# The distance bias of steps 14 to 35: from VectorE's pass over the scores to an identity matmul on PE

## The chip, the cores and the metric

The kernel runs on one core of one Trainium2 chip. The time is the device time of one execution in microseconds. The runs shown take 443.14, 443.22 and 443.57 us, median 443.22 us. The profiled execution took 443.25 us, and its span, from the first to the last instruction, is 441.4 us.

## The reference

A local attention with a few global keys is followed by a gated feed-forward layer with a convolution over time. Batch 4, 8 heads of 64, 768 positions, model width 512, inner width 1024:

```python
scores = scale * np.matmul(q, k.transpose(0, 1, 3, 2))        # scale = 1/8
keep = is_global | is_local                                   # 8 global keys, 96 local ones back
dist = np.where(is_global & ~is_local, float(n_local), np.abs(rel))
scores = scores - slopes[:, None, None] * dist                # slopes 2**-(head + 1)
scores = np.where(keep, scores, -1000000000.0)
a = np.exp(scores - scores.max(-1)); a = a / (a.sum(-1) + 1e-09); o = a @ v
h = np.maximum(x @ w_in, 0.0)                                 # x: the heads' o side by side
conv_out[t] = conv_w[0] * h[t - 1] + conv_w[1] * h[t] + conv_w[2] * h[t + 1]
out = h / (1 + np.exp(-conv_out)) @ w_out
```

`w_in`, `conv_w` and `w_out` come as float64 and are decoded on the chip into two fp32r planes, high and low.

## The kernel before

**Steps.** A batch's 768 queries are cut into two units `u` of 384, a unit into 3 blocks `i` of 128 queries. A job `m` is one pair of heads of one unit of one batch, 32 jobs in all (`jobs`, in the order batch, unit, pair), and a step `s` is one block of one job: 96 steps, `steps[s] = (m, i)`. A step's 128 queries see at most 232 keys (`WIN`: 96 before them, their own 128, 8 global ones); where `u` and `i` are both 0 (`first`) there are 128 (`W0`).

**One step.** `scores(s)` (line 353) writes both heads' scores into one PSUM bank, a tile `both` of 128 x 2 x 256, of which there are two that take turns (`ps_s`). In jobs 0 to 11 (`NATIVE`), which are steps 0 to 35, a head's scores are one fp32 matmul over 64 rows (line 365), which the chip runs as two instructions with a weight load each. Later jobs use planes of fp32r and two matmuls over 128 rows (line 375). `maxima(s)` (line 384) then runs one VectorE instruction per head (line 392): it adds the bias and mask from the table `tab`, multiplies by -0.125, writes the result over the scores, and gives the least value of each row, the negative of the maximum. A short instruction behind it reads the accumulator into `mm`. `exps(s)` (line 399) is one exponential per head on ACT, out of PSUM into a buffer in SBUF (`pbuf`, one of four), with `mm` as its bias and the sums as a by-product. `normalise` (line 417) multiplies by the inverse sums, mostly on POOL (line 427); `transposes` (line 429) turns the blocks on PE (lines 434 and 436) and copies them on ACT; `block` (line 475) multiplies them with the values.

**The table.** `tab` (line 189) holds, in bf16 for each of the 8 heads, 232 + 128 columns of bias times 8, with a very large negative number where a key is masked; `ident` (line 172) is the identity in fp32, used by the transposes.

**The feed-forward half.** `mm1` (line 523) and `mm2` (line 634) are its matmuls in fp32r, three products per tile. They stand in a queue, from which `fill` puts some into each step, so that PE has work besides the attention. Lines 569 to 571 are the convolution (POOL, then VectorE twice).

**Order.** Steps 0 to 13 (`HAND` is 14) are in an order written out by hand (`by_hand`), with warming matmuls in bf16 between them (line 152). From step 14 on a planner orders the instructions of every engine by estimated durations. In steps 14 to 29 (`alone`) the sums get their 1e-9 on POOL (line 420). POOL's queue at the start holds the masks' index tiles, the identity, then the distances (lines 200 and 201), which wait for VectorE, and the tables. At the end the kernel checks that its inputs lie in the range it was written for, and jumps to a general version if not; it isn't taken here.

Of the kernel before, what the change touches and what calls it, by code (L numbers as in the profile page):

```python
# [11 lines left out]
BF16 = mybir.dt.bfloat16  # L12
# [3 lines left out]
ALU = mybir.AluOpType  # L16
# [4 lines left out]
P = 128  # L21
# [4 lines left out]
NB = TB // P  # L26
NPREV, NGLOB = 96, 8
WIN = NPREV + P + NGLOB
# [12 lines left out]
HAND = 14  # L41
FREE = 4
NATIVE = 12
# [17 lines left out]
def key_start(u, i):  # L61
    return (P + NGLOB) * i - (0 if u or i == 0 else P + NGLOB - 32)
# [5 lines left out]
def fast_path(tc, io):  # L68
    nc = tc.nc
    V, A, G, T = nc.vector, nc.scalar, nc.gpsimd, nc.tensor  # L70
# [4 lines left out]
    def pool(name, bufs, **kw):  # L75
        p = tc.tile_pool(name=name, bufs=bufs, **kw)
        pools.append(p)
        return p.__enter__()

    const = pool("const", 1)  # L80
# [90 lines left out]
    G.iota(keyi, pattern=[[1, 64]], base=0, channel_multiplier=0)  # L171
    ident = const.tile([P, P], F32, name="ident")
    make_identity(nc, ident)
    V.tensor_copy(rel, reli)
    keepkey = p1.tile([P, NT + 64], F32, tag="ob", name="keep")
    keep, key = keepkey[:, :NT], keepkey[:, NT:]
# [12 lines left out]
    tab = const.tile([P, H, NT], BF16, name="tab")  # L189
# [151 lines left out]
        V.tensor_tensor(bad, bad, red[:, 1:2], ALU.add)  # L341

    steps = [(m, i) for m in range(len(jobs)) for i in range(NB)]
    last_ttr = {}
    st_s, st_pt, pv, xt, sums = {}, {}, {}, {}, {}

    def alone(s):
        return HAND <= s < NB * (NATIVE - 2)

    def free(s):  # L350
        return s < NB * FREE

    def scores(s):
        m, i = steps[s]
        b, u, hp = jobs[m]
        w = NKC[u]
        first = u == 0 and i == 0
        n = W0 if first else WIN
        k0 = key_start(u, i)
        both = ps_s.tile([P, 2, 256], F32, tag="s", name=f"s{s}")  # L360
        sp = [both[:, 0], both[:, 1]]
        for j in range(2):
            if m < NATIVE:
                rq, rk = raw[m]
                last_mm[s] = T.matmul(  # L365
                    sp[j][:, :n],
                    rq[:D, j * TB + i * P : j * TB + (i + 1) * P],
                    rk[:D, j * w + k0 : j * w + k0 + n],
                    start=True,
                    stop=True,  # L370
                )
                continue
            qh, ql, kk = qk[m]
            for n_, (q_, st, sp_) in enumerate(((qh, True, False), (ql, False, True))):
                last_mm[s] = T.matmul(  # L375
                    sp[j][:, :n],
                    q_[:, j * TB + i * P : j * TB + (i + 1) * P],
                    kk[:, j * w + k0 : j * w + k0 + n],
                    start=st,
                    stop=sp_,  # L380
                )
        st_s[s] = (sp, n, first)

    def maxima(s):
        m, i = steps[s]
        b, u, hp = jobs[m]
        sp, n, first = st_s[s]
        mm = p1.tile([P, 8], F32, tag="mm", name=f"mm{s}", bufs=6)
        for j in range(2):
            h = 2 * hp + j  # L390
            tb = tab[:, h, WIN:] if first else tab[:, h, 0:WIN]
            last_ttr[s] = V.tensor_tensor_reduce(  # L392
                out=sp[j][:, :n], in0=sp[j][:, :n], in1=tb,
                scale=-0.125, scalar=3.0e38, op0=ALU.add, op1=ALU.min,
                accum_out=mm[:, j : j + 1],
            )
        st_s[s] = (sp, n, mm)

    def exps(s):
        m, i = steps[s]  # L400
        sp, n, mm = st_s[s]
        pb = pbuf[s % NPB]
        total = mm[:, 2:4]
        if free(s):
            if i == 0:
                sums[m] = p1.tile([P, 4 * NB], F32, tag="sum", name=f"sum{m}", bufs=2)
            total = sums[m][:, 2 * i : 2 * i + 2]
        for j in range(2):
            last_exp[s] = A.activation(  # L409
                pb[:, j * WIN : j * WIN + n], sp[j][:, :n], AF.Exp,  # L410
                bias=mm[:, j : j + 1], scale=-1.0, accum_out=total[:, j : j + 1],
            )
        st_s[s] = (pb, n, mm)
        if s < SHARED and not alone(s) and not free(s):
            A.activation(mm[:, 4:6], mm[:, 2:4], AF.Identity, bias=eps)
# [288 lines left out]
    last_exp, last_mm, last_ev = {}, {}, {}  # L704
# [69 lines left out]
    def by_hand(s):  # L774
        m, i = steps[s]
        p, q = s - 1, s - 2
        scores(s)
        if q >= 0 and free(q):
            block(*steps[q])
# [6 lines left out]
        if p >= 0 and free(p):  # L786
            transposes(p)
        maxima(s)
        exps(s)
        if ends(s - 3):  # L790
            mixed_low((s - 3) // NB)
# [21 lines left out]
    for s in range(len(steps) + LAG_V + 1):  # L813
# [4 lines left out]
        else:  # L818
# [5 lines left out]
            if s < len(steps):  # L824
                scores(s)
                maxima(s)
                exps(s)
# [207 lines left out]
def build(nc, io):  # L1035
    with tile.TileContext(nc, schedule_with_timeline_sim=True) as tc:
        fast_path(tc, io)
# [50 lines left out]
```

## Time and profile before

| | |
|---|---|
| median of three runs | 443.22 us |
| profiled execution | 443.25 us, span 441.4 us |
| PE, matmuls | 434.3 us busy, 98% of the span |
| PE, weight loads | 375.1 us, 85% |
| VectorE | 345.1 us, 78% |
| ACT | 284.7 us, 65% |
| POOL | 221.9 us, 50% |
| native scores, line 365 | 144 matmuls, steps 0 to 35, 6.8 to 112.6 us |
| bias and maxima, line 392 | 192, 73.1 us busy, mean 382 ns |
| exponentials, line 409 | 192, 82.7 us busy, mean 439 ns |

A matmul's busy time lasts until its modelled end, which lies well behind the start of the next one; what a matmul costs is therefore read from start to start. The weight loads have a row of their own, since they run beside the matmuls before them. An instruction's idle time is put down to what ended it last.

### The profile page before, as it was taken

The numbers are of one execution on the slowest core, as the hardware profiler recorded it, in microseconds if no ns is written. First come the engines' busy times: TensorE is split into PE (matmuls) and PEld (weight loads), VectorE is DVE, ScalarE is ACT, GpSimd is POOL, SyncE is SP. The second block draws the span as 40 slices with busy tenths as digits, with TensorE's granted clock in tenths as the row PEclk, the third lists the DMA queues.
The fourth block names the chain that finished last, engine by engine and source line by source line (L and its number), as shares of the span: only waits on it lengthen the run. The fifth ranks groups of instructions, "written<-read, shape, count | busy, mean of one in ns | idle before, by whom it ended". The sixth has DMA issues, their size and how long they took to land.

```text
span 441.4 us, 8881 instructions
## 1 busy us (share of the span) xinstructions
PE 434.3 (98%) x3014; PEld 375.1 (85%) x3014; DVE 345.1 (78%) x888; ACT 284.7 (65%) x771; POOL 221.9 (50%) x324
## 2 busy tenths in 40 slices
PE   9999999999999999999999999999999999999996
PEld 8677877788879998889989988889989998799885
DVE  5797899979999988857989897857989876666600
ACT  2777698597887875747776676647776675336311
POOL 4311789954834963557656873557656731022000
PEclk9999999999999999999999999999999999999999
DMA  7976855222243334253335234353334366810111
GB/s 218 311 214 192 244 170 166 75 82 84 91 134 131 110 111 133 73 166 105 108 117 164 85 109 134 97 154 98 112 110 135 131 228 231 287 55 1 48 50 53
DMA packets 20837, 58.70 MB, mean 133 GB/s; under 512 B 2736, under 2 KB 2992, under 8 KB 20784
## 3 DMA queue, kind: packets, MB, share of 16 engines
q1 hardware_dynamic: 16960, 51.56, 37.5%
q10 hardware_dynamic: 3824, 6.49, 3.9%
q8 instruction: 26, 0.43, 0.4%
q14 instruction: 27, 0.22, 0.2%
HBM read 51.75 MB, written 6.29 MB: 132 GB/s over the span
## 4 chain that ended last, share of the span: by engine, by line
PE 81%; DVE 7%; POOL 3%; DMA 3%; ACT 3%; issue 1%; SPq 0%; ACTq 0%; DVEq 0%; POOLq 0%
PE o L634 28%; PE h L523 26%; PE pv L485 7%; PE s L375 6%; PE t L434 4%; PE s L365 3%; PE t L436 3%; POOL pbuf L427 2%; DMA wr<-in_w 2%; DVE c L571 2%; DVE s L392 1%; DVE c L570 1%; PE o L904 1%; DMA rq<-in_qk 1%; PE warm L152 1%
## 5 line engine op out<-in xcount | busy, mean ns | idle before, releaser
L427 POOL TENSOR_SCALAR pbuf<-pbuf,mm 128x232 f32<-128x232 f32 (+1 forms) x156 | 108.0, 703 | 82.8 <-DVE mm L421 59.5
L409 ACT ACTIVATE pbuf<-s,mm 128x232 f32<-128x232 f32 (+1 forms) x192 | 82.7, 439 | 52.3 <-DVE mm L392 39.3
L392 DVE CUSTOM_DVE_ANT_0 s<-s,tab 128x232 f32<-128x232 f32 (+1 forms) x192 | 73.1, 382 | 10.2 <-PE s L365 4.0
L634 PE MATMUL o<-woh,gh 128*128 128x512 f32 x184 | 75.4, 410 | 0.0
L634 PE MATMUL o<-wol,gh 128*128 128x512 f32 x184 | 73.3, 398 | 0.0
L634 PE MATMUL o<-woh,gl 128*128 128x512 f32 x184 | 72.9, 397 | 0.0
L569 POOL TENSOR_SCALAR c<-hbuf,cw 128x382 f32<-128x382 f32 (+1 forms) x64 | 47.7, 748 | 47.1 <-ACT hbuf L533 25.0
L439 ACT ACTIVATE pt<-t 128x512 f32<-128x512 f32 (+1 forms) x96 | 53.9, 565 | 12.6 <-PE t L436 10.2
L523 PE MATMUL h<-xh,wih 128*128 128x384 f32 x252 | 59.5, 349 | 0.0
L523 PE MATMUL h<-xl,wih 128*128 128x384 f32 x252 | 57.6, 343 | 0.0
L523 PE MATMUL h<-xh,wil 128*128 128x384 f32 x252 | 56.5, 343 | 0.0
L570 DVE SCALAR_TENSOR_TENSOR c<-hbuf,cw,c 128x382 f32<-128x382 f32 (+1 forms) x64 | 46.4, 732 | 11.2 <-POOL c L569 11.2
L434 PE MATMUL t<-ident,pbuf 128*128 128x128 f32 x192 | 47.1, 275 | 0.3 <-ACT pt L439 0.2
L523 PEld LDWEIGHTS h<-xh,wih 128*128 128x128 f32 x252 | 43.2, 189 | 3.0 <-issue 1.5
L523 PEld LDWEIGHTS h<-xh,wil 128*128 128x128 f32 x252 | 43.5, 188 | 1.7 <-issue 1.2
L571 DVE SCALAR_TENSOR_TENSOR c<-hbuf,cw,c 128x382 f32<-128x382 f32 (+1 forms) x64 | 44.3, 693 | 0.6
L523 PEld LDWEIGHTS h<-xl,wih 128*128 128x128 f32 x252 | 43.1, 189 | 1.4 <-issue 0.9
L533 ACT ACTIVATE hbuf<-h 128x384 f32<-128x384 f32 x64 | 31.1, 493 | 17.9 <-PE h L523 17.8
L485 PEld LDWEIGHTS pv<-pt,v 128*64 128x64 f32 (+1 forms) x664 | 34.0, 136 | 9.5 <-issue 5.6
L589 ACT ACTIVATE c<-c 128x764 f32<-128x764 f32 (+1 forms) x32 | 27.2, 851 | 22.7 <-DVE c L571 19.8
L485 PE MATMUL pv<-pt,v 128*64 128x128 f32 (+1 forms) x664 | 40.9, 268 | 0.5 <-ACT pt L439 0.4
L634 PEld LDWEIGHTS o<-woh,gl 128*128 128x128 f32 x184 | 34.6, 188 | 7.9
(121 smaller groups left out, 851.0 us busy)
## 6 DMA issues: line engine op xcount, KB each, us to landing
v<-in_vv SPq DMA_DIRECT2D x32, 384.0 KB, 3.9
wr<-in_w SPq DMA_DIRECT2D x16, 512.0 KB, 4.6
check<-in_w SPq DMA_DIRECT2D x16, 512.0 KB, 4.6
rq<-in_qk SPq DMA_DIRECT2D x20, 384.0 KB, 3.1
rk<-in_qk SPq DMA_DIRECT2D x12, 504.0 KB, 3.7
out<-ob ACTq DMA_DIRECT2D x23, 256.0 KB, 2.5
rk<-in_qk SPq DMA_DIRECT2D x8, 400.0 KB, 3.3
rq<-in_qk SPq DMA_DIRECT2D x11, 192.0 KB, 5.4
```

The costliest lines, as they stand in the source:

```text
L392: last_ttr[s] = V.tensor_tensor_reduce(out=sp[j][:, :n], in0=sp[j][:, :n], in1=tb, scale=-0.125, scalar=3.0e38, op0=ALU.add, op1=ALU.min, ...
L409: last_exp[s] = A.activation(pb[:, j * WIN : j * WIN + n], sp[j][:, :n], AF.Exp, bias=mm[:, j : j + 1], scale=-1.0, accum_out=total[:, j : ...
L427: G.tensor_scalar(x, x, inv, 1.0, ALU.mult, ALU.mult)
L434: T.transpose(pt[:, 0, j], pb[:, j * WIN : j * WIN + P], ident)
L439: last_ev[s] = A.activation(sb[:, :k], pt[:, :k], AF.Copy)
L485: T.matmul(pv[m][64 * j : 64 * j + 64, i * P + q : (i + 1) * P], vt[m][:n, i, c, 64 * j : 64 * j + 64], sb[:n, c, j, q:], start=c == 0, st ...
L523: T.matmul(ps[:, :TB], w_[:, k, fs], x_, start=part == 0 and k == 0, stop=part == 2 and k == NK - 1,)
L533: A.activation(half, ps[:, :TB], AF.Relu, scale=0.5)
L569: G.tensor_scalar(c, *tap(1), 1.0, ALU.mult, ALU.mult)
L570: V.scalar_tensor_tensor(c, *tap(0), c, ALU.mult, ALU.add)
L571: V.scalar_tensor_tensor(c, *tap(2), c, ALU.mult, ALU.add)
L634: T.matmul(ps, g_[:, f], w_[:, f], start=f == 0 and part == 0, stop=f == NF - 1 and part == 2,)
```

## The change

In steps 14 to 35 (`added`) the head's score matmul no longer closes the sum in PSUM. Behind it stands a bf16 matmul of the 128 x 128 identity with the head's columns of `tab`, which adds the table to the scores and closes it: two such matmuls a step, of 232 columns, or 128 in steps 24, 27, 30 and 33. VectorE then takes the maximum of both heads in one reduction over 128 x 2 x n out of PSUM, writes no scores back, and multiplies the two maxima by -0.125 in a second, tiny operation. The exponentials read the sums in PSUM with a scale of 0.125 in place of -1. The identity in bf16 is copied from the fp32 one by POOL at the start.

```diff
--- before.py
+++ after.py
@@ -171,6 +171,8 @@
     G.iota(keyi, pattern=[[1, 64]], base=0, channel_multiplier=0)
     ident = const.tile([P, P], F32, name="ident")
     make_identity(nc, ident)
+    ident16 = const.tile([P, P], BF16, name="ident16")
+    G.tensor_copy(ident16, ident)
     V.tensor_copy(rel, reli)
     keepkey = p1.tile([P, NT + 64], F32, tag="ob", name="keep")
     keep, key = keepkey[:, :NT], keepkey[:, NT:]
@@ -341,8 +343,11 @@
         V.tensor_tensor(bad, bad, red[:, 1:2], ALU.add)
 
     steps = [(m, i) for m in range(len(jobs)) for i in range(NB)]
-    last_ttr = {}
+    last_ttr, whole = {}, {}
     st_s, st_pt, pv, xt, sums = {}, {}, {}, {}, {}
+
+    def added(s):
+        return HAND <= s < NB * NATIVE
 
     def alone(s):
         return HAND <= s < NB * (NATIVE - 2)
@@ -367,8 +372,13 @@
                     rq[:D, j * TB + i * P : j * TB + (i + 1) * P],
                     rk[:D, j * w + k0 : j * w + k0 + n],
                     start=True,
-                    stop=True,
+                    stop=not added(s),
                 )
+                if added(s):
+                    c0 = WIN if first else 0
+                    last_mm[s] = T.matmul(
+                        sp[j][:, :n], ident16, tab[:, 2 * hp + j, c0 : c0 + n], start=False, stop=True
+                    )
                 continue
             qh, ql, kk = qk[m]
             for n_, (q_, st, sp_) in enumerate(((qh, True, False), (ql, False, True))):
@@ -380,12 +390,20 @@
                     stop=sp_,
                 )
         st_s[s] = (sp, n, first)
+        if added(s):
+            whole[s] = both
 
     def maxima(s):
         m, i = steps[s]
         b, u, hp = jobs[m]
         sp, n, first = st_s[s]
         mm = p1.tile([P, 8], F32, tag="mm", name=f"mm{s}", bufs=6)
+        if added(s):
+            st_s[s] = (sp, n, mm)
+            both = whole.pop(s)
+            V.tensor_reduce(mm[:, 2:4], both[:, :, :n], axis=mybir.AxisListType.X, op=ALU.max)
+            last_ttr[s] = V.tensor_scalar(mm[:, 0:2], mm[:, 2:4], -0.125, None, ALU.mult)
+            return
         for j in range(2):
             h = 2 * hp + j
             tb = tab[:, h, WIN:] if first else tab[:, h, 0:WIN]
@@ -408,7 +426,8 @@
         for j in range(2):
             last_exp[s] = A.activation(
                 pb[:, j * WIN : j * WIN + n], sp[j][:, :n], AF.Exp,
-                bias=mm[:, j : j + 1], scale=-1.0, accum_out=total[:, j : j + 1],
+                bias=mm[:, j : j + 1], scale=0.125 if added(s) else -1.0,
+                accum_out=total[:, j : j + 1],
             )
         st_s[s] = (pb, n, mm)
         if s < SHARED and not alone(s) and not free(s):
```

## Rows read from the trace of the kernel before

**Rows 1.** Chain by engine (page part 4), then by line from 130 us.

```profile
PE 81%; DVE 7%; POOL 3%; DMA 3%; ACT 3%; issue 1%; SPq 0%; ACTq 0%; DVEq 0%; POOLq 0%
...
by line: PE o L634 39.7%; PE h L523 32.6%; PE pv L485 8.6%; PE s L375 8.2%; PE t L434 4.2%; PE t L436 3.6%; PE o L904 1.8%; ACT oc L908 0.1%; PE total L917 0.0%; issue 0.0%
```

**Rows 2.** Busy us by stretch: PE, PEld, DVE, ACT, POOL (instructions); granted clock; DMA.

```profile
44.00:113.00 69.00, 68.19 (x452) 54.97 (x453) 61.82 (x170) 53.39 (x158) 52.02 (x78) 1.00 0.46 143
113.00:130.00 17.00, 16.66 (x109) 14.10 (x110) 16.38 (x36) 14.11 (x37) 9.26 (x12) 1.00 0.26 77
130.00:390.00 260.00, 260.00 (x1813) 231.84 (x1812) 216.32 (x539) 171.97 (x460) 143.77 (x189) 1.00 0.42 137
```

**Rows 3.** Waits on PE, 44-441 us, matmuls and weight loads: us, times, longest.

```profile
PE t L436 <- POOL pbuf L427: 0.4, 1, 0.4
...
PEld s L365 <- ACT pbuf L409: 1.1, 4, 0.4
```

**Rows 4.** PE in time order, a native step and what follows: start, us.

```profile
62.06 0.46 PE L365 MATMUL s<-rk,rq 64*128 64x232 f32 x1
...
62.37 0.55 PE L365 MATMUL s<-rk,rq 64*128 64x232 f32 x2
...
62.56 0.55 PE L365 MATMUL s<-rk,rq 64*128 64x232 f32 x2
...
62.76 0.36 PE L365 MATMUL s<-rk,rq 64*128 64x232 f32 x1
63.04 0.44 PE L523 MATMUL h<-xh,wih 128*128 128x384 f32 x1
...
63.33 0.50 PE L523 MATMUL h<-xh,wih 128*128 128x384 f32 x2
```

**Rows 5.** PE in order of time, where bf16 matmuls stand beside others.

```profile
7.97 0.36 PE L365 MATMUL s<-rk,rq 64*128 64x232 f32 x1
...
8.26 0.51 PE L152 MATMUL warm<-setup 128*128 128x128 bf16 x6
...
22.40 0.33 PE L544 MATMUL h<-xh,wil 128*128 128x384 f32 x1
22.57 0.51 PE L152 MATMUL warm<-setup 128*128 128x128 bf16 x6
22.92 0.28 PE L434 MATMUL t<-ident,pbuf 128*128 128x128 f32 x1
...
41.97 0.22 PE L152 MATMUL warm<-setup 128*128 128x128 bf16 x1
42.12 0.46 PE L365 MATMUL s<-rk,rq 64*128 64x232 f32 x1
```

**Rows 6.** PE in time order, an fp32r score and the group behind.

```profile
116.11 0.28 PE L375 MATMUL s<-kk,ql 128*128 128x232 f32 x1
116.22 0.86 PE L523 MATMUL h<-xl,wih 128*128 128x384 f32 x4
...
116.22 0.34 PE L523 MATMUL h<-xl,wih 128*128 128x384 f32 x1
```

**Rows 7.** VectorE in time order, then groups by form: busy us, mean ns.

```profile
50.58 0.41 DVE L392 CUSTOM_DVE_ANT_0 s<-s,tab 128x232 f32<-128x232 f32 x1 [1.82 <-PE s L365]
...
51.08 0.41 DVE L392 CUSTOM_DVE_ANT_0 s<-s,tab 128x232 f32<-128x232 f32 x1
...
L392 DVE CUSTOM_DVE_ANT_0 s<-s,tab 128x232 f32<-128x232 f32 x160 | 63.7, 400 | 7.8 <-PE s L365 3.5 <-PE s L375 2.1 <-POOL tab L205 0.8
...
L421 DVE RECIPROCAL mm<-mm 128x2 f32<-128x2 f32 x84 | 13.3, 159 | 3.0 <-POOL mm L420 1.4 <-ACT mm L415 0.9
...
L333 DVE TENSOR_REDUCE misc<-acc 128x1 f32<-128x512 f32 x1 | 0.7, 687 | 0.0
```

**Rows 8.** ACT in order of time, the first exponential of step 16.

```profile
51.64 0.45 ACT L409 ACTIVATE pbuf<-s,mm 128x232 f32<-128x232 f32 x1 [1.26 <-POOL c L569]
```

**Rows 9.** POOL in order of time, its first operation on the masks' distances.

```profile
7.50 0.38 POOL L200 TENSOR_SCALAR keep<-loc 128x232 f32<-128x232 f32 x1 [5.22 <-DVE loc L199]
```

## The prediction

> **What bounds the kernel now.** I read the chain of waits first, then the busy time by stretch, then PE's waits, then single instructions in the stretch of steps 14 to 35. The chain [rows 1] is 81% PE with 7% of VectorE and 3% each of POOL and ACT; the pieces that are not PE lie ahead of 130 us, so the chain alone would let one think that VectorE or POOL sets the pace in the steps that are changed. The busy time by stretch says otherwise [rows 2]. From 44 to 113 us, where the scores of steps 14 to 35 run, PE is busy 68.19 of 69.00 us, VectorE 61.82, POOL 52.02. From 113 to 130 us PE is busy 16.66 of 17.00 us, and from 130 to 390 us all 260 us. PE's idle time from 44 to 390 us is thus 0.81 + 0.34 = 1.15 us. The waits of PE's matmuls from 44 us to the end agree: the longest is 0.4 us [rows 3]. PE has ready work of the feed-forward half to put in wherever a score or a transpose is late, so the last instruction comes when PE's list is done. What is added to PE's list after 44 us comes out at the end, less what it fills of 1.15 us of idle time.
>
> PE's busy time is modelled, so the price of an instruction is read from start to start of neighbours. One step of native scores with 232 columns [rows 4]: its four matmuls (two per head) start at 62.06, 62.37, 62.56 and 62.76, the next group's first two at 63.04 and 63.33. The gaps are 0.31, 0.19, 0.20, 0.28 and 0.29 us. The middle ones, 0.19 to 0.20, are the matmul itself. The others are longer: the first by 0.11, the fourth by 0.09, and the fifth by 0.12 against the 0.17 at which matmuls of that form follow one another (from 116.22, four of them in 0.86 us, each lasting 0.34: three gaps in 0.52) [rows 6]. What distinguishes those places is the form of the tile: the native scores are 64\*128 (64 rows of the array), their neighbours 128\*128. It isn't the type: from an fp32r matmul to a bf16 one, both 128\*128, the gap is 0.17 (22.40 to 22.57), and six bf16 pairs and the step to an fp32 transpose take 0.35 together, 0.058 each [rows 5]. But from a 64-row score to a bf16 128\*128 matmul it is 0.29 (7.97 to 8.26), and from a bf16 one to a 64-row score 0.15 (41.97 to 42.12) in place of 0.058 [rows 5]. So a change between 64 and 128 rows costs 0.09 us before it and some 0.11 us at the first pair behind it, unless that one is bf16 (the six from 8.26 take 0.51, the last of them 0.22: 0.058 from one to the next).
>
> The Trainium skill has a rule for this: TensorEngine Tiling (Array Packing), section Key Properties, says that changing the tiling mode, not merely the tile, drains the engine. It gives no figure; the trace agrees, at 0.09 us a change. It speaks against this change, whose identity has 128 rows and stands between scores of 64.
>
> **PE's part.** Each of the 22 steps gets two bf16 matmuls, identity by table. 18 steps have 232 columns, 4 (steps 24, 27, 30, 33) have 128. A bf16 pair of 128 columns takes 0.058 [rows 5]; 104 columns more at the granted clock of 1.00, the upper level of 2.4 GHz [rows 2], are 0.043, so 0.10, and the fp32r pairs of 232 columns that already run take 0.11 [rows 6]. From a step's first score to the second matmul behind the step:
> before 0.31 + 0.19 + 0.20 + 0.28 + 0.29 = 1.27;
> after 0.31 (head 0) + 0.29 (to the identity) + 0.19 (0.10 and 0.09 back to 64 rows) + 0.31 (head 1, its first weights exposed again) + 0.29 (to the identity) + 0.11 (to the next group, no change of form) + 0.17 = 1.67.
> The difference is 0.40 us. With 128 columns it is 0.40 - 2 x 0.043 = 0.31. The sum is 18 x 0.40 + 4 x 0.31 = 8.4 us. Bounds: 4.4 us if the changes of form cost nothing (36 x 0.11 + 8 x 0.058); at the most 8.4 + 22 x 0.11 = 10.8 us, if the first pair behind each step still pays as it does now. I take 8.4, since each of its gaps is a row with the same two forms.
>
> What it fills: PE's own idle time from 44 to 113 us, 0.81 us. VectorE, POOL and ACT get 8 us more for the same work, so I let PE's waits there go: -0.8. As lower bound, none of it goes; as upper, the 1.15 us.
>
> **VectorE's part.** Off: two maxima per step, 0.40 us each with 232 columns [rows 7], 0.82 to 0.91 for the pair back to back (50.58 to 51.08, and 0.41). On: one reduction over 464 columns. The nearest row is a reduction of 512 columns from SBUF, 0.687; 464/512 of it is 0.62, and I take 0.64, between the two. And a 128x2 scalar operation, 0.16 like the reciprocal of that size [rows 7]. Together 0.80 (0.78 to 0.85) where the pair had 0.80 to 0.91: VectorE loses 0.05 or gains 0.13 us a step, likely 0.1, some 2 us in all. That is off the path, as PE's idle time is what it could remove: already counted.
>
> **What becomes later.** The first maximum could start when head 0's second matmul had ended, 0.31 + 0.36 = 0.67 after the step's first one, and the pair ended 0.50 + 0.41 behind that, at 1.58; the exponentials followed the second maximum (51.08 + 0.41, and 51.64) [rows 7, 8]. Now the reduction waits for the second identity, which starts 0.31 + 0.29 + 0.19 + 0.31 + 0.29 = 1.39 after the first matmul and lasts some 0.27; with 0.80 for both operations the exponentials can start at 2.46, 0.9 later. Behind them stand the inverse, POOL's normalising and the transposes, three steps on, and the score bank: two banks turn, so the scores of step s+2 wait for the exponentials of s. That wait occurs 4 times now, 1.1 us of weight-load idle time in all [rows 3]. If each of the four were 0.9 longer it would be 3.6 us; but two steps of PE also become 2 x 0.40 = 0.8 longer, which covers nearly all of it. I take 0, with 3.6 as the upper end.
>
> **The rest.** POOL's copy of the identity to bf16 stands ahead of an operation before which POOL sits idle for 5.22 us [rows 9]: nothing. The planner orders everything from step 14 on anew from its own costs; it can't shorten PE's list, only shift where PE waits: 0, within about 1 us either way, by the 1.15 us that there is now. No DMA is added or moved past a queue. Sum: +8.4 - 0.8 = +7.6 us on the profiled execution's 443.25 us (span 441.4), 0.03 above the runs' median of 443.22: 450.9.
>
> **Rivals.**
> Columns only: the array takes the identity without the price of the form, between heads as well; 4.4 - 0.8 gives 446.9. For it: the bf16 pairs in a row cost their columns only. Against: both mixed gaps of rows 5. The Trainium skill's page TensorE: Matmul & The Clock Gate, section Back-to-back issue gap, would have it so: columns over 2.4 GHz plus 2.5 ns, an estimate of 0.099 and 0.056 us, 4.0 us in all; the rows of 64-row neighbours contradict it here.
> Faster, because VectorE sets the pace: if the chain's VectorE pieces are the true path from 44 to 130 us, the pairs on PE fall into time in which PE only does work ahead, and VectorE's 22 x 0.1 us come off: 441.0. It needs about 8 us of slack on PE ahead of 130 us; rows 2 show 1.15. It decides if modelled ends hide idle time in PE's busy.
> No change: POOL's normalising (75% busy from 44 to 113 us) sets the pace, PE's price is hidden and VectorE's gain too: 443.2. Against: the same 1.15 us.
> Late banks: the longer way to the exponentials stops PE at the score banks: 450.9 + 3.6 = 454.5.
>
> **How the numbers follow.** Full price 0.66 (449.5 to 452.5), columns only 0.13, late banks 0.06, faster 0.09, no change 0.06. The predicted time is that of the first, 450.9. The range, 446.6 to 453.4, takes in the second and leaves out the others, 0.21. Within 0.2% (0.9 us) is about what a measurement of this kernel can tell from no change. Faster 0.09, same 0.06, slower 0.85.
>
> **What would show it.** In a changed step the gap from a score to the identity should be 0.29, from the identity to head 1's first score 0.19, and 0.31 behind that; from the second identity to the next group 0.11. Step 36's last score, now at 116.11 [rows 6], should start some 7 to 8 us later, and everything behind it keep its length, with PE still busy all of its time. Reductions should take 0.62 to 0.69 us. I am wrong if these gaps stand near 0.10, if PE's list grows by 8 us and the end does not move, or if PE shows long waits for exponentials.

## The result

The changed kernel takes 449.60 us (median of four runs, 449.50 to 450.31), the kernel before 443.39 us (443.14 to 443.68, the runs beside it among them): a ratio of 1.0146, 95% interval 1.0133 to 1.0159, some 6.2 us slower. The profiled execution took 449.50 us, span 447.7 us; 6.25 us more than the one before.

### The profile page after: what moved, and what is told of

The parts are those of the page before. It is cut to its first block, busy times and chain, and to the rows that moved or that the text cites. A ratio compares the mean times of both kernels' runs of the same rounds, so it can differ in the third digit from the quotient of the medians.

```text
span 447.7 us, 8935 instructions
## 1 busy us (share of the span) xinstructions
PE 441.9 (99%) x3058; PEld 377.0 (84%) x3058; DVE 345.3 (77%) x844; ACT 285.0 (64%) x771; POOL 224.3 (50%) x325
## 4 chain that ended last, share of the span: by engine, by line
PE 95%; DMA 3%; ACT 1%; DVE 0%; issue 0%; SPq 0%; ACTq 0%
PE h L542 30%; PE o L653 29%; PE pv L504 8%; PE s L370 7%; PE s L385 6%; PE t L453 5%; PE t L455 4%; PE s L379 2%; DMA wr<-in_w 2%; PE o L923 1%; DMA rq<-in_qk 1%; PE warm L152 1%; PE h L563 1%; PE spare L504 1%; PE warm L479 1%; ACT pt L458 0%
## 5 line engine op out<-in xcount | busy, mean ns | idle before, releaser
L446 POOL TENSOR_SCALAR pbuf<-pbuf,mm 128x232 f32<-128x232 f32 (+1 forms) x156 | 106.4, 692 | 86.0 <-DVE mm L440 55.8
L588 POOL TENSOR_SCALAR c<-hbuf,cw 128x382 f32<-128x382 f32 (+1 forms) x64 | 49.4, 776 | 48.6 <-ACT hbuf L552 26.3
L410 DVE CUSTOM_DVE_ANT_0 s<-s,tab 128x232 f32<-128x232 f32 (+1 forms) x148 | 56.8, 385 | 8.8 <-PE s L385 5.1
L589 DVE SCALAR_TENSOR_TENSOR c<-hbuf,cw,c 128x382 f32<-128x382 f32 (+1 forms) x64 | 45.4, 717 | 10.0 <-POOL c L588 10.0
L590 DVE SCALAR_TENSOR_TENSOR c<-hbuf,cw,c 128x382 f32<-128x382 f32 (+1 forms) x64 | 43.3, 681 | 0.5
```

The source lines that it names most:

```text
L410: last_ttr[s] = V.tensor_tensor_reduce(out=sp[j][:, :n], in0=sp[j][:, :n], in1=tb, scale=-0.125, scalar=3.0e38, op0=ALU.add, op1=ALU.min, ...
L446: G.tensor_scalar(x, x, inv, 1.0, ALU.mult, ALU.mult)
L588: G.tensor_scalar(c, *tap(1), 1.0, ALU.mult, ALU.mult)
L589: V.scalar_tensor_tensor(c, *tap(0), c, ALU.mult, ALU.add)
L590: V.scalar_tensor_tensor(c, *tap(2), c, ALU.mult, ALU.add)
```

## The profile after

The chain by engine (page part 4), which answers to [rows 1]:

```profile
PE 95%; DMA 3%; ACT 1%; DVE 0%; issue 0%; SPq 0%; ACTq 0%
```

Then busy time by stretch, as in [rows 2] (PE, PEld, VectorE, ACT, POOL; granted clock; DMA), and the weight loads' wait that answers to [rows 3]; from 44 us on there is no wait of a PE matmul left to show:

```profile
44.00:113.00 69.00, 69.00 (x461) 51.55 (x459) 57.12 (x118) 49.94 (x143) 45.83 (x73) 1.00 0.42 125
113.00:130.00 17.00, 17.00 (x110) 13.93 (x106) 16.85 (x33) 13.34 (x40) 12.59 (x13) 1.00 0.35 107
130.00:390.00 260.00, 260.00 (x1818) 231.48 (x1817) 215.72 (x544) 174.93 (x469) 148.25 (x193) 1.00 0.42 135
```

```profile
PEld s L370 <- ACT pbuf L427: 0.4, 2, 0.2
```

PE is now busy all of the time from 44 to 390 us, and the chain is PE alone but for the start. The 1.15 us of idle time are gone.

One changed step of 232 columns on PE in order of time (line 370 the scores, 379 the identities, 542 the feed-forward half), which answers to [rows 4], and the last score of step 36, which answers to [rows 6]:

```profile
52.46 0.66 PE L370 MATMUL s<-rk,rq 64*128 64x232 f32 x2
53.05 0.27 PE L379 MATMUL s<-tab,ident 128*128 128x232 bf16 x1
53.25 0.66 PE L370 MATMUL s<-rk,rq 64*128 64x232 f32 x2
53.84 0.27 PE L379 MATMUL s<-tab,ident 128*128 128x232 bf16 x1
53.88 0.60 PE L542 MATMUL h<-xh,wih 128*128 128x384 f32 x2
...
125.30 0.27 PE L385 MATMUL s<-kk,ql 128*128 128x232 f32 x1
```

The first identity starts 0.59 behind the step's first score: 0.30 and 0.29. From there to head 1's first score it is 0.20, then again 0.59 to the second identity. The feed-forward group's first two start 0.04 and 0.30 behind that (two in 0.60, the last lasting 0.34). Step 36's last score moved from 116.11 to 125.30.

VectorE, by form and in order of time, answering to [rows 7]: the reduction (line 404), the scalar operation (405), and what stands behind each:

```profile
L404 DVE TENSOR_REDUCE mm<-s 128x2 f32<-128x464 f32 x18 | 11.4, 633 | 6.6 <-PE s L379 6.5
...
L405 DVE TENSOR_SCALAR mm<-mm 128x2 f32<-128x2 f32 x22 | 5.3, 241 | 0.3
...
54.41 0.63 DVE L404 TENSOR_REDUCE mm<-s 128x2 f32<-128x464 f32 x1
54.96 0.61 DVE L589 SCALAR_TENSOR_TENSOR c<-hbuf,cw,c 128x382 f32<-128x382 f32 x1
...
56.14 0.16 DVE L405 TENSOR_SCALAR mm<-mm 128x2 f32<-128x2 f32 x1
56.21 0.87 DVE L310 TENSOR_TENSOR wil<-w,wih 128x512 fp32r<-128x512 f32 x1
```

The reduction holds the queue for 0.55 (54.41 to 54.96), the scalar operation for some 0.07 where other work lies between. In the kernel before, a maximum with other work behind it held it for 0.32, so the pair for 0.64:

```profile
55.16 0.40 DVE L392 CUSTOM_DVE_ANT_0 s<-s,tab 128x232 f32<-128x232 f32 x1
...
55.48 0.68 DVE L308 TENSOR_TENSOR wil<-w,wih 128x512 fp32r<-128x512 f32 x1
```

With 0.62 for 0.64, VectorE's list got no shorter to speak of.

From the first score of step 14, which starts at 42.12 us in both traces, to the last matmul it is 395.02 us before and 401.36 after. Summing the gaps from start to start by the group that the earlier matmul belongs to (all of PE's matmuls, as in the fence above):

| PE from step 14 on, us | before | after | |
|---|---|---|---|
| native scores, 88 | 20.72 | 24.52 | +3.80 |
| identities, 44 | 0 | 5.26 | +5.26 |
| transposes, 312 | 31.17 | 29.73 | -1.45 |
| feed-forward, first half, 759 | 140.80 | 139.81 | -1.00 |
| feed-forward, second half, 599 | 139.23 | 138.99 | -0.24 |
| values, fp32r scores, the rest | 63.09 | 63.06 | -0.04 |

The list gained 9.06 us where the steps are. Priced by the step it is the same: from the first score to the second matmul behind the step it is 1.68 where it was 1.26 with 232 columns, and 1.29 where it was 0.92 with 128, so 18 x 0.42 + 4 x 0.37 = 9.0. And 2.7 us went from gaps of other groups, most of it waits, such as the 0.67 from one transpose to the next at 66.15 us of the kernel before, where 0.11 is usual. The busy times show 0.40 of that 0.56 as idle:

```profile
66.15 0.27 PE L434 MATMUL t<-ident,pbuf 128*128 128x128 f32 x1
66.82 0.33 PE L436 MATMUL t<-ident,pbuf 128*128 128x128 f32 x1 [0.40 <-POOL pbuf L427]
66.98 0.27 PE L434 MATMUL t<-ident,pbuf 128*128 128x128 f32 x1
67.09 0.27 PE L436 MATMUL t<-ident,pbuf 128*128 128x128 f32 x1
```

## Experiments

The theory after the result: PE's list sets the end; the changes between 64 and 128 rows are the larger half of what it gained; VectorE's part lies off the path (it does not move the end). The first rival: it isn't the form, but any further matmul in the sum. The second: VectorE's relief is what gave the 2.7 us back.

**1. Zero weights of 128 rows, VectorE as before**

```diff
# against the kernel before; nil16 is a 128 x 128 tile of bf16 zeros
-                    stop=True,
+                    stop=not added(s),
                 )
+                if added(s):
+                    c0 = WIN if first else 0
+                    last_mm[s] = T.matmul(
+                        sp[j][:, :n], nil16[:P], tab[:P, 2 * hp + j, c0 : c0 + n],
+                        start=False, stop=True,
+                    )
```

> The kernel before, with VectorE's two maxima as they were, and behind each head's scores of steps 14 to 35 a bf16 matmul of 128 rows by the same table columns as in the change, whose weights are zero: it adds nothing. PE's list is the changed kernel's, VectorE's that of before. Theory (PE's list sets the end, the changes between 64 and 128 rows are more than half of what it gained, VectorE is off the path): 449.6 us, 448.8 to 450.4, with gaps of 0.29 from a score to the added matmul and 0.20 from it to the next score. Rival (VectorE's relief is what gave back the 2.7 us that PE's other groups lost in the changed kernel): 451 to 452.3 us.

Measured: 449.69 us, ratio 1.0149 (1.0132 to 1.0166). One step on PE, where 379 is the added matmul:

```profile
52.50 0.66 PE L370 MATMUL s<-rk,rq 64*128 64x232 f32 x2
53.09 0.27 PE L379 MATMUL s<-tab,nil 128*128 128x232 bf16 x1
53.29 0.66 PE L370 MATMUL s<-rk,rq 64*128 64x232 f32 x2
53.88 0.27 PE L379 MATMUL s<-tab,nil 128*128 128x232 bf16 x1
53.92 0.95 PE L534 MATMUL h<-xh,wih 128*128 128x384 f32 x4
```

The gaps are those of the changed kernel, and so is the time, with VectorE's work untouched. PE's other groups lost 3.0 us here: 1.35 in the feed-forward's first half, 1.30 in the transposes, 0.38 in the second half. So PE's longer list is enough to give back the 2.7 us, and the second rival falls.

**2. The same with 64 rows**

```diff
# against run 1
-                        sp[j][:, :n], nil16[:P], tab[:P, 2 * hp + j, c0 : c0 + n],
+                        sp[j][:, :n], nil16[:D], tab[:D, 2 * hp + j, c0 : c0 + n],
```

> As the run with zero weights of 128 rows, but the added matmuls take only rows 0 to 63 of the zero weights and of the table, so that they have the scores' own form, 64*128. Number, columns, type and place in the sum are the same. Theory (the form is what costs): gaps of 0.20 from a score to the added matmul, 0.10 to 0.20 from it to the next score, no second 0.30; 0.2 to 0.3 us a step in place of 0.42; 444.7 to 446.7 us. Rival (any further bf16 matmul that adds to an fp32 sum costs this, whatever its rows): 449.6 us, as with 128 rows.

Measured: 445.72 us, ratio 1.0060 (1.0043 to 1.0076), 4.0 us less than with 128 rows, for the same number of matmuls, columns and types.

```profile
51.79 0.66 PE L370 MATMUL s<-rk,rq 64*128 64x232 f32 x2
52.28 0.26 PE L379 MATMUL s<-tab,nil 64*128 64x232 bf16 x1
52.38 0.56 PE L370 MATMUL s<-rk,rq 64*128 64x232 f32 x2
52.79 0.26 PE L379 MATMUL s<-tab,nil 64*128 64x232 bf16 x1
52.98 0.97 PE L534 MATMUL h<-xh,wih 128*128 128x384 f32 x4
```

From head 0's second score to the added matmul it is now 0.20 (51.79 and 0.30 and 0.20), from that to head 1's first score 0.10, and the gap behind, which was 0.30, is 0.21. The added matmul costs its columns; the 0.09 is paid once, behind the second one (52.79 to 52.98). The form is the cause, and the first rival falls. A step's gaps grew by 0.21 here (with 128 columns by 0.16), some 4.4 us in all, of which 2.5 show in the time.

The 0.10 agrees with what the Trainium skill's page TensorE: Matmul & The Clock Gate, section Back-to-back issue gap, gives as the gap of an isolated matmul: 0.099 for 232 columns, an estimate by it; run 1, where the form changes behind the same matmul, has 0.20. Runs 1 and 2 also agree with the rule of the Trainium skill's page TensorEngine Tiling (Array Packing), section Key Properties, that a change of tiling mode drains the engine: they show what a change costs, 0.09 to 0.10 us, and not the draining itself.

**3. One identity for both heads, ahead of the scores**

```diff
# against the changed kernel; the identities behind the scores are taken out
+        if added(s):
+            c0 = WIN if first else 0
+            T.matmul(
+                both[:, :, :n], ident16, tab[:, 2 * hp : 2 * hp + 2, c0 : c0 + n], start=True, stop=False
+            )
-                    start=True,
-                    stop=not added(s),
+                    start=not added(s),
+                    stop=j == 1 or not added(s),
```

> The changed kernel with one identity matmul over both heads' 464 columns, put ahead of the two scores, which add to it: as many columns as in the change, but no change of form between the heads, only the two per step that there were before. VectorE as in the change. Theory: PE gains about 0.19 to 0.22 us a step, 4.0 us in all, and its other groups lose up to 2.7 as they did: 444.4 to 447.4 us. Rival (the added columns and loads cost the same wherever they stand): 449.6 us.

Measured: 444.85 us, ratio 1.0038 (1.0025 to 1.0050).

```profile
51.79 0.37 PE L369 MATMUL s<-tab,ident 128*128 128x464 bf16 x1
52.09 1.05 PE L375 MATMUL s<-rk,rq 64*128 64x232 f32 x4
53.07 0.97 PE L542 MATMUL h<-xh,wih 128*128 128x384 f32 x4
```

As many columns as in the change; the identity takes 0.30 with the change to the scores in it, of which 0.20 is new (ahead of it stood the same change). The order, with one matmul for two, is worth 4.8 us, and the change still loses.

**4. Two reductions in place of one**

```diff
# against the changed kernel
-            V.tensor_reduce(mm[:, 2:4], both[:, :, :n], axis=mybir.AxisListType.X, op=ALU.max)
+            for j in range(2):
+                V.tensor_reduce(mm[:, 2 + j : 3 + j], sp[j][:, :n], axis=mybir.AxisListType.X, op=ALU.max)
```

> The changed kernel, but the maxima of steps 14 to 35 are two reductions of 232 columns, one per head, in place of one of 464. PE's list is the same; VectorE gets about 0.2 us more per step, 4 us in all. Theory (VectorE is off the path): 449.6 us, 448.9 to 450.4. Rival (the one reduction is worth its time): 451 to 453 us.

Measured: 449.53 us, ratio 1.0140 (1.0124 to 1.0157): as the changed kernel. The reductions, by form:

```profile
L405 DVE TENSOR_REDUCE mm<-s 128x1 f32<-128x232 f32 x36 | 12.7, 390 | 6.6 <-PE s L379 6.4
```

Two of 390 ns for one of 633 do not move the end, and no gain of the one reduction shows in this kernel. The test is a small one, though: from start to start the two hold VectorE for 0.62 where the one holds it for 0.55, so the run added 0.07 us a step, 1.5 us in all, and not the 4 that were expected.

**5. No change of form at all: scores over 128 rows, without identities**

```diff
# against the kernel before; wide(m): 5 <= m < NATIVE and m % NPAIR
-        n = D if m < NATIVE else P
+        n = D if m < NATIVE and not wide(m) else P
...
+                K = P if wide(m) else D
...
-                    rq[:D, j * TB + i * P : j * TB + (i + 1) * P],
-                    rk[:D, j * w + k0 : j * w + k0 + n],
+                    rq[:K, j * TB + i * P : j * TB + (i + 1) * P],
+                    rk[:K, j * w + k0 : j * w + k0 + n],
...
-            tb = tab[:, h, WIN:] if first else tab[:, h, 0:WIN]
+            k = h - 1 if wide(m) else h
+            tb = tab[:, k, WIN:] if first else tab[:, k, 0:WIN]
...
-                scale=-0.125, scalar=3.0e38, op0=ALU.add, op1=ALU.min,
+                scale=-0.0625 if wide(m) else -0.125, scalar=3.0e38, op0=ALU.add, op1=ALU.min,
```

> The kernel before, with the native scores of 18 steps (jobs 5, 6, 7, 9, 10, 11) over 128 rows instead of 64: the host's arrays hold each head's planes twice, both copies are loaded, so that a product is twice the score; VectorE adds the table of the head before, which is twice this head's, and multiplies by -0.0625. No bias on PE. Theory (a change between 64 and 128 rows costs 0.09 us ahead and 0.10 to 0.11 us behind): each such step loses both of its changes, 0.39 us, 7 us in all; PE then waits more for VectorE, POOL and ACT, whose work is unchanged, up to some 4 us: 436.3 to 440.5 us. Rival (the long gaps belong to native fp32 scores as such, or loading both copies holds the start up): 443.3 us or more.

Measured: 442.53 us, ratio 0.9984 (0.9975 to 0.9993). Faster (every run lies below every one of the kernel before beside it), but by 0.6 us of the medians, not by 3 to 7: a miss. One step on PE (the last line, from a narrower window, is its third and fourth score):

```profile
70.31 0.95 PE L369 MATMUL s<-rk,rq 128*128 128x232 f32 x4
70.93 0.86 PE L528 MATMUL h<-xh,wih 128*128 128x384 f32 x3
...
70.71 0.56 PE L369 MATMUL s<-rk,rq 128*128 128x232 f32 x2
```

The gaps did go: four scores and the first matmul behind them in 0.62 where [rows 4] has 0.98, and the gap after that is 0.34 where it was 0.29. But the time did not. PE's longest waits from 40 to 130 us, and the stretch that holds the most of them, here and then in the kernel before:

```profile
PE s L369 <- ACT pbuf L414: 2.1, 3, 1.5
PE t L439 <- POOL qh L137: 1.3, 1, 1.3
PE t L441 <- POOL pbuf L432: 0.8, 2, 0.6
...
60.00:75.00 15.00, 12.23 (x82) 10.01 (x81) 14.95 (x44) 12.07 (x36) 12.83 (x20) 1.00 0.67 221
```

```profile
60.00:75.00 15.00, 14.50 (x92) 10.86 (x91) 14.96 (x44) 12.15 (x36) 12.84 (x20) 1.00 0.59 197
```

PE is idle for 2.77 of 15 us from 60 to 75, where VectorE is busy 14.95. It was as full there in the kernel before, 14.96, where PE showed 0.50 idle. From 44 to 130 us PE's idle time is 5.22 us (the sum over five stretches), against 1.15 before. What PE's list lost came back as waits, none of them on a load. By these numbers PE's list and the chain of the other engines were about equally long in the kernel before: 9.0 us more on the list show as 6.3 at the end, and 7 us less as 0.6. Which engine that other chain hangs on, this run does not show.

**6. The changed kernel with scores over 128 rows**

```diff
# against the changed kernel: the edits of run 5 to the loads and the scores, both scales halved in those 18 steps, and
-                        sp[j][:, :n], ident16, tab[:, 2 * hp + j, c0 : c0 + n], start=False, stop=True
+                        sp[j][:, :n], ident16, tab[:, 2 * hp + j - (1 if wide(m) else 0), c0 : c0 + n], start=False, stop=True
```

> The changed kernel with the scores of the same 18 steps over 128 rows, so that score and identity have one form there (the identity adds the table of the head before, and the scale is 0.0625). Theory: in these steps the identity costs its columns, 0.2 to 0.24 us a step, and no change of form is left; 18 x (0.42 + 0.39 - 0.22) = 10.6 us less than 449.6 for PE's list, some of it taken back by waits: 439.0 to 443.5 us. Rival (the identity's place in the sum costs, not the form): 442.6 us of gain from the scores' own changes alone, with gaps of 0.29 and 0.20 still there around the identity.

(The rival's figure stands for a time of 442.6 us.) Measured: 443.24 us, ratio 1.0003 (0.9994 to 1.0013), at the upper end of the theory's range; the gaps decide against the rival:

```profile
54.79 0.56 PE L374 MATMUL s<-rk,rq 128*128 128x232 f32 x2
55.19 0.26 PE L383 MATMUL s<-tab,ident 128*128 128x232 bf16 x1
55.28 0.57 PE L374 MATMUL s<-rk,rq 128*128 128x232 f32 x2
55.69 0.26 PE L383 MATMUL s<-tab,ident 128*128 128x232 bf16 x1
55.72 0.77 PE L546 MATMUL h<-xh,wih 128*128 128x384 f32 x3
```

From score to identity 0.20 (0.40 from 54.79, of which 0.20 is head 0's own first gap), from identity to score 0.09 to 0.10. The identity of the change costs nothing but its columns here, and the 6.2 us are gone, with the help of the scores' own changes of form, which went as in run 5.

**7 to 9. Who holds PE once its list is shorter**

```diff
# against run 5 (run 7), the kernel before (run 8) and run 6 (run 9)
-            if j and s < SHARED and not alone(s):
+            if j and s < SHARED and (s % 2 or not alone(s)):
```

> The kernel of the run with 128-row scores (442.5 us), and in every odd step of 15 to 29 the second head's normalising goes to ACT instead of POOL, as it does already in steps 30 to 39. PE's list stays. Theory (what PE lost in its list came back as waits on POOL's chain of normalising from 57 to 92 us): POOL's chain gets some 0.7 us a step shorter in 8 steps, 438 to 441.5 us. Rival (the waits are on something else, VectorE's decoding or the score banks, or ACT's order now holds the exponentials up): 442.5 us or more.

> The same edit alone on the kernel before, as a control. Theory (there PE's list has only 1 to 2.7 us of waits in it): 441.5 to 443.3 us. Rival (POOL set the pace of the kernel before as well): below 441 us.

> The same edit on the changed kernel with 128-row scores (443.2 us): PE's list is longer by the identities' columns, VectorE's shorter. Theory (POOL's chain holds PE there as well, though less, since its list is longer): 441 to 443 us, not below the same edit without identities. Rival (VectorE holds the stage once POOL is relieved, and the reduction relieves it): below the same edit without identities.

Measured: 442.60 us (0.9983, 0.9974 to 0.9992; the theory's range missed by 1.1), 443.46 us (1.0007, 0.9998 to 1.0016; missed by 0.2) and 441.70 us (0.9977, 0.9963 to 0.9991). Waits of PE's scores, and of the exponentials for VectorE's maxima, from 40 to 130 us in run 7, then in run 9:

```profile
PE s L369 <- ACT pbuf L414: 3.5, 5, 1.0
PE s L379 <- ACT pbuf L414: 1.0, 1, 1.0
...
ACT pbuf L414 <- DVE mm L397: 8.6, 9, 2.4
```

```profile
PE s L374 <- ACT pbuf L431: 1.4, 2, 1.1
...
ACT pbuf L431 <- DVE mm L409: 3.7, 6, 1.1
```

Relieving POOL does nothing by itself: PE's waits moved from transposes to the score banks, whose exponentials were late. So my theory of POOL fell. With the identity and the one reduction as well, these waits are down from 4.5 to 1.4 us, and the time is the lowest so far; by the medians that is the rival's side. The exponentials' own waits for the maxima fell with them, from 8.6 to 3.7 us, which speaks for VectorE; but the intervals of runs 7 and 9 overlap, and whether it is VectorE's shorter work or the planner's new order was not settled.

**10 and 11. Identities only where the form is one**

```diff
# run 10, against run 9
-        return HAND <= s < NB * NATIVE
+        return HAND <= s < NB * NATIVE and wide(s // NB)
# run 11, against run 10: the one identity of both heads ahead of the scores, as in run 3
```

> The kernel of the run at 441.7 us (changed, 128-row scores, normalising shared with ACT), with the identities only in the 18 steps whose scores have 128 rows; the other 4 of steps 14 to 35 are as before. Theory: those 4 steps lose 0.42 us each of PE's list, 1.7 us, of which waits may take up to all: 440.0 to 441.7 us. Rival (VectorE's relief in those 4 steps is worth more than PE's price): above 441.9 us.

> The same, with one identity matmul of both heads' columns ahead of the two scores in place of one behind each. Both have one form, so neither place costs a change; theory: one load and one short matmul less per step, 0 to 0.06 us, and the reduction starts up to 0.1 us earlier, as the last score ends the sum: 439.5 to 441.7 us, within 0.8 of the run beside it. Rival (the place in the sum counts by itself): over 1 us apart.

Measured: 441.70 us (0.9957, 0.9932 to 0.9981) and 442.04 us (0.9963, 0.9940 to 0.9987; the theory's range missed by 0.3). Both beat the kernel before, by 1.6 and 1.2 us of the medians. Run 10 is no faster than run 9: of the 1.7 us that its four steps took off PE's list nothing shows. In run 11 the identity, its scores and the group behind stand like this:

```profile
61.24 0.36 PE L373 MATMUL s<-tab,ident 128*128 128x464 bf16 x1
61.44 0.95 PE L380 MATMUL s<-rk,rq 128*128 128x232 f32 x4
62.05 1.03 PE L547 MATMUL h<-xh,wih 128*128 128x384 f32 x4
```

The identity of 464 columns takes 0.20 and nothing is added behind it. In PE's gaps the place costs nothing where the form is one, and the two runs lie 0.3 apart, within the 0.8 that was expected.

## Why the prediction was right

The time, 449.6 us, lies 1.3 below the 450.9 that was forecast and within the likeliest case's own 449.5 to 452.5.

- *PE's list sets the end.* Right for a list that grows: no PE wait is left from 44 us on, and run 1 has the same time with VectorE's work as before. Run 4 says little more, as it added only 1.5 us to VectorE.
- *The price of the form.* Right: 0.29 from score to identity, 0.30 behind the return (forecast 0.31), 0.30 from the second identity to the second matmul behind the step (forecast 0.28). The return itself is 0.20, not 0.19. Run 2 shows it with 4.0 us less for 64 rows in place of 128, and run 6 from the other side, with 128 rows for all.
- *The sum.* 9.06 us measured for scores and identities where 8.4 was forecast, as the steps of 232 columns cost 0.42 and not 0.40, and those of 128 columns 0.37 and not 0.31.
- *What it fills.* The term that was mis-sized: -0.8 forecast, about -2.7 measured, outside the bounds of 0 to 1.15 that were given for it. I took PE's idle time from the busy times, whose modelled ends lie over the gap behind them and hide waits; the gaps from start to start show more. The two errors, +0.6 and -1.9, have opposite signs; that they leave only 1.3 us is luck.
- *VectorE.* Off the path as forecast; the gain of 0.1 us a step is not there from start to start (0.62 for 0.64).
- *What becomes later.* Right at 0: no PE wait for the score banks, and their weight loads wait 0.4 us, not 1.1. But the reason was another than the one given: the exponentials did not start 0.9 later. From a step's first score to its first exponential the traces have 3.68 us before and 3.57 after (medians of the 22 steps); the two VectorE operations do not stand back to back, as the sum took them, but 1.73 apart in the step above, with other work between.
- *Step 36.* A sign that was missed: its last score came 9.2 us later, not 7 to 8, and from there to the last matmul it took 318.2 us and not 321.0. In the new order 194 feed-forward matmuls stand ahead of it where there were 184.
- *Rivals.* Columns only is what run 2 and run 6 make of the kernel; in the change itself it does not hold. Faster through VectorE and no change through POOL: the result excludes both, since the end moved with PE's list. Late banks: no such wait.

What I had not weighed: the same rows said that the native scores pay for two changes of form in each step already. Run 5 removes them, and shows that at the end they were not worth their 7 us either.

## What to carry to other kernels

Price an added matmul from neighbours of its own form and from a pair of both forms, not from its columns: put between two matmuls of another row count, it cost about twice its columns here, and the same matmul ahead of both, or of the same row count, costs its columns alone. A list that is full and a chain that is just as long look the same in busy time; here a longer list showed at the end for the most part, a shorter one nearly not at all. That a longer chain of the other engines would show too was not run. Read an engine's waits from start to start where the ends are modelled.

## What the runs showed of the hardware

A matmul of one form behind another of the same form may have its start recorded 0.03 to 0.04 us behind it, with the missing time in the next gap: 0.04 and 0.26 behind the second identity, 0.03 and 0.34 behind the 128-row scores of run 5 (0.20 for the score and 0.17 for the matmul behind it give the same sum). So the sum of the two was taken as the price. A native fp32 score of 232 columns takes 0.20 a matmul with 64 and with 128 rows alike. And a stage with PE busy 99% of its time gave back 0.6 of about 7 us when PE's list was cut.
